# GateLoop attention with a maxout FFN: weight blocks fetched between the first gates' inputs and rounded ahead of the second group, the first FFN done block by block, and the second group without GpSimd

## Chip, cores, metric

One core of one Trainium2 chip. Times are device microseconds (us) of one execution; a median over a few executions is quoted with its lowest and highest.

## The reference

```python
# B, H, S, D = 4, 8, 768, 48
scale = np.minimum(mag, 0.999) / (mag + 1e-06)      # mag = |a|
for t in range(S):
    new_re = ar * S_re - ai * S_im                  # a complex state per head, D x D
    new_im = ar * S_im + ai * S_re
    S_re, S_im = new_re + k[t] (outer) v[t], new_im
    y[t] = q[t] @ S_re
x = y as (3072, 384)
h = max(x @ w1, x @ w2, x @ w3)                     # 384 -> 768
return h @ w_out                                    # 768 -> 384
```

The weights come as float64. The kernel reads each value as two int32 words and rounds it to float32 itself.

## The kernel before

The 3072 tokens are 24 tiles of 128. Two tiles are a group: group 0 is tiles 0 and 1, group 1 tiles 2 and 3, group 2 tiles 4 and 5. A group passes through *gates* (logarithm and angle of each a), *products* (decay of k and q), *angles* (prefix sums of the angles on TensorE, then sines), and then, for each tile, a *front* (transposes `turn`, decay factors `cut`, and `prep`, which makes Q, K, QB, KB, QG), the scores, the state and the outputs. An FFN step works a weight block against a tile's (later a group's) outputs. Tiles 0 and 1 have an FFN each, called FFN 0 and FFN 1 here; later FFNs take two tiles.

The gates:

```python
def gate_steps(g, cs):                      # cs: chunks (tiles) of the group
    def s0():
        # ... cut ...
        nc.scalar.activation(out=w, in_=ar, func=AF.Square)
        nc.scalar.activation(out=L, in_=ai, func=AF.Square)
        nc.vector.tensor_tensor(out=L, in0=L, in1=w, op=OP.add)
        nc.vector.tensor_scalar(out=L, in0=L, scalar1=SMALL, scalar2=LARGE, op0=OP.max, op1=OP.min)
        act(out=L, in_=L, func=AF.Ln)
    # ... s1 cut ...
    def s2():
        # ... cut ...
        (nc.gpsimd if g > 0 else nc.vector).tensor_tensor(out=ai, in0=ai, in1=L, op=OP.mult)
        nc.vector.tensor_tensor(out=w, in0=w, in1=L, op=OP.mult)
        nc.vector.scalar_tensor_tensor(out=w, in0=w, scalar=2.0, in1=ai, op0=OP.subtract, op1=OP.mult)
        # ... cut ...
    return [s0, s1, s2]
```

The rounding of one weight block, right behind its load:

```python
def load_weight(dst, src, i):
    # ... choice of the raw buffer cut ...
    nc.sync.dma_start(out=raw.rearrange("p n m w -> p n (m w)"), in_=src.bitcast(I32))
    low, high = raw[:, :, :, 0].bitcast(U32), raw[:, :, :, 1]
    ex = fp2.tile([P, n, m], I32, tag="xT", name="ex")
    nc.vector.tensor_scalar(out=ex, in0=high, scalar1=0x7FF00000, scalar2=None, op0=OP.bitwise_and)
    nc.scalar.activation(out=ex, in_=ex, func=AF.Relu, scale=8.0, bias=wbias)
    nc.vector.scalar_tensor_tensor(out=ex, in0=high, scalar=-0x80000000, in1=ex,
                                   op0=OP.bitwise_and, op1=OP.bitwise_or)
    nc.vector.tensor_scalar(out=high, in0=high, scalar1=0x000FFFFF, scalar2=None, op0=OP.bitwise_and)
    nc.scalar.activation(out=dst, in_=high, func=AF.Copy, scale=2.0 ** -20, bias=1.0)
    nc.vector.scalar_tensor_tensor(out=dst, in0=low, scalar=2.0 ** -52, in1=dst, op0=OP.mult, op1=OP.add)
    nc.vector.tensor_tensor(out=dst, in0=dst, in1=ex.bitcast(FP), op=OP.mult)
```

The order of the program. `weave` merges lists of steps, each over a stretch of the whole (0 to 1):

```python
load(0); load_v(0)
constants_early()                            # small masks on GpSimd
for t in us["k"] + us["q"] + fs + gs + vbs[2:]:
    nc.gpsimd.memset(t, 0.0)                 # the run of zero fills
weights = weight_steps()
# ... gates of group 0, chunk by chunk, and its first products ...
for f in weights[:3]: f()                    # blocks 0 to 2: load and round
load(1)
angles(0, list(range(C)))
# ... front of tile 0 ...
for g in range(NG):
    load_v(g + 1); load(g + 2)
    if g == 0:
        weave((0.0, 1.0, loop_steps(0)), (0.0, 0.7, weights[3:]), (0.15, 0.58, pre_steps(1)), (0.7, 1.0, ffn_steps([0])))
    else:
        ffn = ffn_steps(tokens(g * C - 1))
        # ...
        weave((0.0, 1.0, loop_steps(g)), (0.0, 0.7, pre_steps(g + 1, feed)),
              (0.0, 1.0 if g > 1 else 0.5, [call(feed, 1) for _ in ffn]))
```

So before, the gates and angles of group 1 are worked beside group 0's tiles, together with the rounding, and FFN 1 is spread over group 1's loop.

Of the kernel before, what the change touches and what calls it, by code (L numbers as in the profile page):

```python
# [9 lines left out]
FP = mybir.dt.float32  # L10
# [35 lines left out]
def kernel(  # L46
# [167 lines left out]
    def rows(a, g, c, lo=0, n=P):  # L214
        b, s = divmod(g, GB)
        t0 = (s * C + c) * P + lo
        return a[b, :, t0:t0 + n, :].rearrange("h t d -> t h d")

    def load(g):
        if g >= NG:  # L220
            return
        for nm, src in (("ar", a_re), ("ai", a_im)):
            T[nm, g] = ld2.tile([P, C, H, D], FP, tag=nm, name=nm)
        for c in range(C):
            for nm, src in (("ar", a_re), ("ai", a_im)):
                nc.sync.dma_start(out=T[nm, g][:, c], in_=rows(src, g, c))  # L226
        for c in range(C):
            x = g * C + c
            for nm, src in (("k", k), ("q", q)):
                T[nm, x] = ldx.tile([P, H, D], FP, tag=nm, name=nm)  # L230
                nc.sync.dma_start(out=T[nm, x], in_=rows(src, g, c))

    def load_v(g):
        if g >= NG:
            return
        for c in range(C):
            x = g * C + c
            T["v", x] = vbs[x % 4]
            for h in range(2):
                src = rows(v, g, c, h * L64, L64).rearrange("t (i u) d -> t i u d", u=2)  # L240
                for u in range(2):
                    nc.sync.dma_start(out=heads(T["v", x][h * L64:(h + 1) * L64, h])[:, :, u], in_=src[:, :, u])

    ws = [const.tile([P, KD, FF], FP, name="w%d" % i) for i in range(3)]
    wo = const.tile([P, KF, DM], FP, name="wo")

    def weight_steps():

        steps, n = [], FF // 3
        for f in range(3):  # L250
            for w, src in zip(ws, (moe_w1, moe_w2, moe_w3)):
                cols = slice(f * n, (f + 1) * n)
                steps.append(call(load_weight, w[:, :, cols], src.rearrange("(i p) m -> p i m", p=P)[:, :, cols], len(steps)))
        for f in range(0, KF, 2):
            view = moe_w_out.rearrange("(i p) m -> p i m", p=P)
            steps.append(call(load_weight, wo[:, f:f + 2], view[:, f:f + 2], 0))
        return steps

    def load_weight(dst, src, i):
        if src.dtype == FP:  # L260
            nc.sync.dma_start(out=dst, in_=src)
            return

        n, m = dst.shape[1:]
        if i % 3 == 2:

            raw = wo.bitcast(I32).rearrange("p f m -> p (f m)")[:, 0:2 * n * m].rearrange("p (n m w) -> p n m w", n=n, w=2)
        else:
            raw = fp2.tile([P, n, m, 2], I32, tag="hT", name="raw")
        nc.sync.dma_start(out=raw.rearrange("p n m w -> p n (m w)"), in_=src.bitcast(I32))  # L270
        low, high = raw[:, :, :, 0].bitcast(U32), raw[:, :, :, 1]

        ex = fp2.tile([P, n, m], I32, tag="xT", name="ex")
# [9 lines that stand above are left out]
# [9 lines left out]
    def gate_steps(g, cs):  # L292
# [27 lines left out]
        def s2():  # L320

            L, w, e, ar, ai = part("L"), part("w"), part("e"), part("ar"), part("ai")
            nc.scalar.activation(out=e, in_=ar, func=AF.Abs)
            nc.vector.tensor_tensor(out=w, in0=w, in1=e, op=OP.add)
            act(out=L, in_=w, func=AF.Ln)
            act(out=L, in_=L, func=AF.Exp, scale=-1.0)

            (nc.gpsimd if g > 0 else nc.vector).tensor_tensor(out=ai, in0=ai, in1=L, op=OP.mult)  # L328
            nc.vector.tensor_tensor(out=w, in0=w, in1=L, op=OP.mult)
            nc.vector.scalar_tensor_tensor(out=w, in0=w, scalar=2.0, in1=ai, op0=OP.subtract, op1=OP.mult)  # L330

            nc.scalar.activation(out=ar, in_=ar, func=AF.Sign, bias=tiny)
            nc.scalar.activation(out=ai, in_=ar, func=AF.Copy, scale=-0.25, bias=0.25)
            nc.scalar.activation(out=ar, in_=ar, func=AF.Copy, scale=-1.0 / math.pi)
            if lo == 0 and g % GB > 0:
                nc.gpsimd.tensor_tensor(out=ai[0:1, 0:DM], in0=ai[0:1, 0:DM], in1=T["carry", g], op=OP.subtract)
# [53 lines left out]
    def products(x):  # L390
        g, c = divmod(x, C)

        def sums(mat, nm):
            ps = psM.tile([P, DM], FP, tag="mm", padded_shape=[P, 512], name=nm)
            nc.tensor.matmul(out=ps, lhsT=mat, rhs=T["Ln", g][:, c * DM:(c + 1) * DM], start=True, stop=True)  # L395
            return ps

        def s0():

            ps = sums(mid, "mds")  # L400
            for nm, sg in (("k", 1.0), ("q", -1.0)):
                E = nat2.tile([P, DM], FP, tag="E", name="E")
                act(out=E, in_=ps, func=AF.Exp, scale=sg)
                eng = nc.gpsimd if g > 0 else nc.vector
                eng.tensor_tensor(out=hd(T[nm, x]), in0=E, in1=hd(T[nm, x]), op=OP.mult)  # L405

        def s1():
            for nm in "kq":
                u = T["U" + nm, x] = us[nm][x % len(us[nm])]
                nc.vector.tensor_tensor(out=u[:, :, :, 0:D], in0=T["CS", x], in1=two(hd(T[nm, x])), op=OP.mult)  # L410

        def s2():

            ps = sums(rest, "sfx")
            En = nat2.tile([P, DM], FP, tag="E", name="En")
            act(out=En, in_=ps, func=AF.Exp, scale=-1.0)
            u = T["Uk", x][:, :, :, 0:D]
            nc.vector.tensor_tensor(out=u, in0=u, in1=two(En), op=OP.mult)

        return s0, s1, s2  # L420


# [120 lines left out]
    def outputs(x, xs):  # L543
# [14 lines left out]
                                 lhsT=V[:, c, i, lo:lo + 32] if new else G[0:DD, c, i, lo:lo + 32],  # L558
                                 rhs=atm[:, h] if new else QG[0:DD, 2 * h + c], start=start, stop=stop)
        if x == xs[0]:  # L560
            T["xT", xs[-1]] = fp2.tile([P, KD, len(xs) * P], FP, tag="xT", padded_shape=[P, KD, TG], name="xT")
        o = (x - xs[0]) * P
        nc.scalar.copy(out=T["xT", xs[-1]][:, :, o:o + P], in_=y)  # L563

# [1 line left out]
    def up_step(xs, fp, i):  # L566
        xT, n = T["xT", xs[-1]], len(xs) * P
        if fp == 0 and i == 0:
            T["hT", xs[-1]] = fp2.tile([P, KF, n], FP, tag="hT", padded_shape=[P, KF, TG], name="hT")
        dst = T["hT", xs[-1]][:, 2 * fp:2 * fp + 2]  # L570
        ps = psM.tile([P, 2, n], FP, tag="mm", padded_shape=[P, 2, TG], name="up")
        for j in range(2):
# [19 lines left out]
    def call(f, *a):  # L592
        return lambda: f(*a)
# [18 lines left out]
        return [call(turn, x, 0), call(turn, x, 1)], [call(cut, x)], \  # L612
            [call(prep, x, p) for p in range(4)]

    def loop_steps(g):
        steps = []
        for x in range(g * C, (g + 1) * C):
            tr, ct, pr = front(x + 1)
            kt = [products(x + 1)[2]] if x + 1 < NX else []
            steps += [call(scores, x, "A"), call(gather, x, "A"), call(scores, x, "B")] + tr[:1]  # L620
            steps += [call(gather, x, "B"), call(state, x)] + tr[1:] + ct + pr[:1] + kt
            steps += [call(outputs, x, tokens(x))] + pr[1:]
        return steps

    table("natural_log_exp_and_others")
    for t in vbs[:2]:
        nc.gpsimd.memset(t, 0.0)
    load(0)
    load_v(0)
    constants_early()  # L630
    for t in us["k"] + us["q"] + fs + gs + vbs[2:]:
        nc.gpsimd.memset(t, 0.0)
    weights = weight_steps()
    for pair in zip(*(gate_steps(0, [c]) for c in range(C))):
        for f in pair:
            f()
    for c in range(C):
        products(c)[0]()
    for f in weights[:3]:
        f()  # L640
    load(1)
    angles(0, list(range(C)))
    constants_late()
    for f in [products(0)[1]] + sum(front(0), []) + [products(0)[2], products(1)[1]]:
        f()
    for g in range(NG):
        load_v(g + 1)
        load(g + 2)
        if g == 0:
            weave((0.0, 1.0, loop_steps(0)), (0.0, 0.7, weights[3:]), (0.15, 0.58, pre_steps(1)), (0.7, 1.0, ffn_steps([0])))  # L650
        else:
            ffn = ffn_steps(tokens(g * C - 1))

            def feed(n):
                for _ in range(min(n, len(ffn))):
                    ffn.pop(0)()

            weave((0.0, 1.0, loop_steps(g)), (0.0, 0.7, pre_steps(g + 1, feed)),
                  (0.0, 1.0 if g > 1 else 0.5, [call(feed, 1) for _ in ffn]))
    for f in ffn_steps(tokens(NX - 1)):  # L660
        f()

# [29 lines left out]
```

## Time and profile before

Before: 751.06 us median of 3 (749.87 to 751.43).

The prediction below shows the page and the stretches. A list of milestones of the profiled run, each the start of a TensorE group in its timeline:

| milestone | before |
|---|---|
| first prefix sum of group 0 | 34.24 |
| first prefix sum of group 1 | 88.1 |
| tile 2's first score product | 109.2 |
| first prefix sum of group 2 | 153.8 |
| tile 3's first score product | 155.9 |
| tile 4's first score product | 167.66 |
| end of the span | 748.2 |

How to read it: the last 580 us are TensorE's and the same in all kernels here, so a kernel is as fast as its tile 4 is early. And at the very start come the second chunk's addition and clamp. These are lines of VectorE's timeline before, and then of GpSimd's. A line of a timeline gives start and duration in us, engine, line of the kernel, operation, and in brackets the idle time before it and what ended it; PE is TensorE, DVE VectorE, ACT ScalarE and POOL GpSimd, and x2 is two instructions in one line.

```profile
7.57 0.56 DVE L307 TENSOR_TENSOR L<-L,w 128x384 f32<-128x384 f32 x1 [1.13 <-ACT L L306]
8.16 0.37 DVE L308 TENSOR_SCALAR L<-L 128x384 f32<-128x384 f32 x1
```

```profile
7.94 2.29 POOL L120 TENSOR_SCALAR_AFFINE_SELECT cuts<-cuts 128x4 f32<-128x4 f32 x14
10.17 1.83 POOL L632 MEMSET uk<- 128x1024 f32 x2
```

### The profile page before, as it was taken

The numbers are of one execution on the slowest core, as the hardware profiler recorded it, in microseconds if no ns is written. First come the engines' busy times: TensorE is split into PE (matmuls) and PEld (weight loads), VectorE is DVE, ScalarE is ACT, GpSimd is POOL, SyncE is SP. The second block draws the span as 40 slices with busy tenths as digits, with TensorE's granted clock in tenths as the row PEclk, the third lists the DMA queues.
The fourth block names the chain that finished last, engine by engine and source line by source line (L and its number), as shares of the span: only waits on it lengthen the run. The fifth ranks groups of instructions, "written<-read, shape, count | busy, mean of one in ns | idle before, by whom it ended". The sixth has DMA issues, their size and how long they took to land.

```text
span 748.2 us, 17645 instructions
## 1 busy us (share of the span) xinstructions
PE 670.9 (90%) x7620; PEld 543.1 (73%) x7620; DVE 518.4 (69%) x706; ACT 402.2 (54%) x677; POOL 130.4 (17%) x133
## 2 busy tenths in 40 slices
PE   1166279989999999999999999999999999999998
PEld 0054168968778878878878868878878878788785
DVE  4889997787866866866856867867857767655210
ACT  7595565666647546556556556556566465322010
POOL 9302400411302203102103103103004005000000
PEclk9986699999999999999999999999999999999999
DMA  9764430050220320320320420410410210000000
GB/s 173 156 178 136 121 92 23 8 103 10 54 65 11 56 66 9 74 51 7 72 54 6 77 52 5 91 35 7 91 33 10 46 33 2 1 23 2 12 11 22
DMA packets 134158, 38.91 MB, mean 52 GB/s; under 512 B 126784, under 2 KB 129856, under 8 KB 134080
## 3 DMA queue, kind: packets, MB, share of 16 engines
q1 hardware_dynamic: 133824, 37.76, 22.8%
q8 instruction: 60, 0.98, 0.6%
q14 instruction: 18, 0.15, 0.1%
q10 hardware_dynamic: 256, 0.01, 0.0%
HBM read 33.03 MB, written 4.72 MB: 50 GB/s over the span
## 4 chain that ended last, share of the span: by engine, by line
PE 73%; issue 11%; DVE 7%; ACT 4%; POOL 2%; SPq 2%; DMA 1%; ACTq 0%; POOLq 0%; DVEq 0%
PE up L575 35%; PE op L586 12%; PE tp L432 5%; PE dk L529 4%; PE B L492 4%; PE y L557 3%; PE A L492 2%; PE mds L395 2%; PE sfx L395 2%; PE F L445 2%; PE cs L350 2%; ACT e L106 1%; DVE QB L459 1%; SPq L226 1%; POOL ai L328 1%
## 5 line engine op out<-in xcount | busy, mean ns | idle before, releaser
L575 PE MATMUL up<-xT,w 128*128 128x256 f32 (+1 forms) x1404 | 299.3, 367 | 6.5 <-ACT xT L563 6.2
L575 PEld LDWEIGHTS up<-xT,w 128*128 128x128 f32 x1404 | 249.0, 191 | 46.4 <-ACT xT L563 7.7
L328 POOL TENSOR_TENSOR ai<-ai,L 128x768 f32<-128x768 f32 x11 | 30.4, 2759 | 418.4 <-ACT L L106 314.1
L586 PE MATMUL op<-wo,hT 128*128 128x384 f32 x288 | 97.9, 490 | 0.0
L580 DVE TENSOR_TENSOR hT<-hT,up 128x512 f32<-128x512 f32 (+1 forms) x78 | 49.9, 640 | 40.0 <-PE up L575 39.8
L586 PEld LDWEIGHTS op<-wo,hT 128*128 128x128 f32 x288 | 52.9, 190 | 33.3 <-DVE hT L580 0.5
L459 DVE TENSOR_TENSOR Q<-Q,f 112x512 f32<-112x512 f32 x48 | 40.3, 840 | 44.9 <-ACT f L106 44.9
L434 ACT COPY K<-tp 112x512 f32<-112x512 f32 x48 | 27.9, 581 | 60.0 <-PE tp L432 59.8
L578 ACT COPY hT<-up 128x512 f32<-128x512 f32 (+1 forms) x39 | 21.3, 548 | 69.6 <-PE up L575 68.6
L588 ACT COPY ot<-op 128x384 f32<-128x384 f32 x24 | 11.5, 477 | 81.5 <-PE op L586 81.5
L541 DVE TENSOR_TENSOR g<-g,dk 112x384 f32<-112x384 f32 x40 | 22.1, 552 | 47.0 <-PE dk L529 46.4
L350 PE MATMUL cs<-w,upto 128*128 128x384 f32 x48 | 20.5, 555 | 34.5 <-DVE w L346 34.5
L529 PEld LDWEIGHTS dk<-vb,uk 128*112 128x112 f32 x384 | 42.7, 183 | 9.9 <-issue 5.5
L557 PEld LDWEIGHTS y<-atm,vb 128*32 128x32 f32 x1536 | 39.7, 112 | 13.5 <-issue 8.4
L529 PE MATMUL dk<-vb,uk 128*112 128x96 f32 x384 | 43.1, 267 | 6.0 <-issue 5.2
L557 PE MATMUL y<-atm,vb 128*32 128x64 f32 x1536 | 47.1, 224 | 0.4 <-DVE atm L510 0.4
L557 PE MATMUL y<-QG,g 112*32 112x64 f32 x1536 | 46.5, 222 | 0.0
L459 DVE TENSOR_TENSOR QB<-Q,f 112x512 f32<-112x512 f32 (+1 forms) x48 | 46.3, 999 | 0.0
L405 POOL TENSOR_TENSOR k<-E,k 128x384 f32<-128x384 f32 x22 | 30.2, 1372 | 68.9 <-ACT E L106 65.2
L492 PE MATMUL A<-Q,K 112*64 112x96 f32 x768 | 38.7, 254 | 3.7 <-DVE Q L459 3.1
L492 PEld LDWEIGHTS A<-Q,K 112*64 112x64 f32 x768 | 33.9, 140 | 9.4 <-issue 5.2
L106 ACT ACTIVATE f<-F 48x296 f32<-48x296 f32 x96 | 39.6, 412 | 1.7 <-PE F L445 0.4
(107 smaller groups left out, 1126.9 us busy)
## 6 DMA issues: line engine op xcount, KB each, us to landing
ar<-in_a_re_dram SPq DMA_DIRECT2D x24, 192.0 KB, 3.6
ai<-in_a_im_dram SPq DMA_DIRECT2D x24, 192.0 KB, 4.0
k<-in_k_dram SPq DMA_DIRECT2D x24, 192.0 KB, 3.0
q<-in_q_dram SPq DMA_DIRECT2D x24, 192.0 KB, 3.0
vb<-in_v_dram SPq DMA_DIRECT2D x96, 48.0 KB, 2.4
raw<-in_moe_w_dram SPq DMA_DIRECT2D x6, 768.0 KB, 5.6
out_dram<-ot SPq DMA_DIRECT2D x24, 192.0 KB, 1.9
wo<-in_moe_w_dram SPq DMA_DIRECT2D x3, 768.0 KB, 6.4
```

The lines of the kernel that those rows point to most:

```text
L106: tab(nc.scalar.activation(**kw))
L328: (nc.gpsimd if g > 0 else nc.vector).tensor_tensor(out=ai, in0=ai, in1=L, op=OP.mult)
L350: nc.tensor.matmul(out=ps, lhsT=upto, rhs=w[:, c * DM:(c + 1) * DM], start=True, stop=c == 0)
L405: eng.tensor_tensor(out=hd(T[nm, x]), in0=E, in1=hd(T[nm, x]), op=OP.mult)
L432: nc.tensor.transpose(out=tp[0:DD, j], in_=both(T["U" + nm, x], hg * HU + j), identity=ident)
L459: nc.vector.tensor_tensor(out=out, in0=in_, in1=f.to_broadcast([DD, H, 2 * n, 8]), op=OP.mult)
L492: nc.tensor.matmul(out=ps[o:o + L64, h // HU, h % HU * 96:h % HU * 96 + 96], lhsT=K[0:DD, h, o:o + L64], rhs=Q[0:DD, 2 * h + c], start=Tru ...
L529: nc.tensor.matmul(out=ps[0:DD, h // HU, h % HU * 96:h % HU * 96 + 96], lhsT=both(T["Uk", x], h), rhs=T["v", x][:, :, h // 2, o:o + D], st ...
L557: nc.tensor.matmul(out=y[32 * (r % 4):32 * (r % 4) + 32, r // 4, c * L64:(c + 1) * L64], lhsT=V[:, c, i, lo:lo + 32] if new else G[0:DD, c ...
L575: nc.tensor.matmul(out=ps[:, j], lhsT=ws[i][:, d, f * P:(f + 1) * P], rhs=xT[:, d], start=(d == 0), stop=(d == KD - 1))
L580: nc.vector.tensor_tensor(out=dst, in0=dst, in1=ps, op=OP.max)
L586: nc.tensor.matmul(out=ps, lhsT=hT[:, f, o:o + P], rhs=wo[:, f], start=(f == 0), stop=(f == KF - 1))
```

## The change

The intent: the first weight blocks come in while the first gates are worked, so that all rounding is done before group 1 instead of running into it; FFN 0 starts while TensorE idles; and group 1's multiplies leave slow GpSimd. Three parts, cut to their core (the split of `load_weight` into `weight_load` and `weight_round`, the smaller load functions and the buffers for `raw`, `xT` and `hT` are left out):

```diff
-            (nc.gpsimd if g > 0 else nc.vector).tensor_tensor(out=ai, in0=ai, in1=L, op=OP.mult)
+            (nc.gpsimd if g > 1 else nc.vector).tensor_tensor(out=ai, in0=ai, in1=L, op=OP.mult)
...
-                eng = nc.gpsimd if g > 0 else nc.vector
+                eng = nc.gpsimd if g > 1 else nc.vector
...
-    load(0)
-    load_v(0)
+    blocks = weight_blocks()
+    for c in range(C):
+        load_a(0, c)
+        weight_load(c)
+    load_kq(0, 0)
+    weight_load(2)
+    load_kq(0, 1)
+    load(0, load_v)
+    for i in range(3, 7):
+        weight_load(i)
...
-    for f in weights[:3]:
-        f()
-    load(1)
+    for i in range(3):
+        weight_round(i)
+    load(1, load_a)
...
-            weave((0.0, 1.0, loop_steps(0)), (0.0, 0.7, weights[3:]), (0.15, 0.58, pre_steps(1)), (0.7, 1.0, ffn_steps([0])))
+    rounds = []
+    for i in range(3, len(blocks)):
+        rounds.append(call(weight_round, i))
+        if i + 4 < len(blocks):
+            rounds.append(call(weight_load, i + 4))
+    weave((0.0, 1.0, tile_steps(0)), (0.0, 1.0, rounds[:8]))
+    load(1, load_kq)
+    load(1, load_v)
+    ffn = ffn_steps([0])
+    weave((0.0, 1.0, ffn[:6] + rounds[8:12] + ffn[6:9] + rounds[12:] + ffn[9:]), (0.3, 1.0, gate_steps(1, list(range(C)))))
+    for f in tile_steps(1, False):
+        f()
+    ffn = ffn_steps([1])
...
+    weave((0.0, 1.0, pre_steps(1, feed)[3:] + sum(front(C), []) + [products(C)[2]]), (0.0, 1.0, [call(feed, 1)] * 5))
```

After it, group 1's gates stand behind most of the rounding, its angles and front behind tile 1, and FFN 1 is used up beside that front. The loops of groups 2 and later are as before.

## The prediction

> **What bounds the kernel now.** I read the page first, then busy time by stretch, then the VectorE and TensorE timelines of the first 170 us.
>
> ```profile
> span 748.2 us, 17645 instructions
> PE 670.9 (90%) x7620; PEld 543.1 (73%) x7620; DVE 518.4 (69%) x706; ACT 402.2 (54%) x677; POOL 130.4 (17%) x133
> ...
> PE   1166279989999999999999999999999999999998
> ...
> DVE  4889997787866866866856867867857767655210
> ...
> PEclk9986699999999999999999999999999999999999
> ```
>
> Each digit is 18.7 us. TensorE (PE) has 9s from the seventh slice on; before that it idles, at a reduced clock, while VectorE (DVE) has 8s and 9s. The averages (PE 90%) hide two kernels: a VectorE-bound start and a TensorE-bound rest. Stretches make that exact (busy us of each engine, then granted clock, DMA share, GB/s):
>
> ```profile
> 0.00:34.00 34.00, 3.27 (x4) 1.00 (x4) 21.46 (x47) 22.23 (x39) 23.69 (x67) 1.00 0.83 168
> 34.00:74.00 40.00, 26.81 (x318) 20.51 (x318) 36.84 (x53) 29.64 (x48) 3.02 (x1) 0.74 0.56 156
> 74.00:82.30 8.30, 0.00 (x0) 0.00 (x0) 6.70 (x5) 4.19 (x6) 6.32 (x5) 0.75 0.37 106
> 82.30:112.00 29.70, 18.52 (x166) 15.19 (x166) 29.61 (x43) 19.00 (x32) 2.18 (x1) 0.79 0.45 107
> 112.00:167.70 55.70, 53.33 (x788) 44.98 (x786) 43.59 (x66) 34.39 (x60) 10.42 (x6) 0.97 0.21 44
> 167.70:748.00 580.30, 569.00 (x6348) 461.41 (x6348) 380.23 (x497) 292.75 (x496) 84.72 (x54) 1.00 0.17 35
> ```
>
> From 167.7 us on PE is 98% busy at full clock: nothing in the start can shorten those 580 us, only move where they begin. I chose 167.7 because there the first score product of tile 4 (group 2) runs, and from that matmul on the PE order of the changed kernel is instruction for instruction that of the old one. So the question is one number: when does that product start?
>
> ```profile
> 167.66 1.54 PE L492 MATMUL A<-Q,K 112*64 112x96 f32 x32 [0.67 <-DVE Q L459]
> ```
>
> It waits for VectorE's Q. VectorE's queue is in order, and carries gates, the rounding of twelve float64 weight blocks (seven instructions each, five of them VectorE's), and the tiles. The worst place in it is where GpSimd takes part (start, duration):
>
> ```profile
> 70.98 4.59 POOL L328 TENSOR_TENSOR ai<-ai,L 128x768 f32<-128x768 f32 x1 [45.76 <-ACT L L106]
> 75.53 0.99 POOL L405 TENSOR_TENSOR k<-E,k 128x384 f32<-128x384 f32 x1
> ...
> 75.60 1.73 DVE L330 SCALAR_TENSOR_TENSOR w<-w,ai 128x768 f32<-128x768 f32 x1 [1.69 <-POOL ai L328]
> 77.26 1.74 DVE L282 TENSOR_TENSOR w<-w,ex 128x768 f32<-128x768 f32 x1
> 78.93 1.75 DVE L418 TENSOR_TENSOR uk<-uk,En 128x768 f32<-128x768 f32 x1
> 80.59 1.74 DVE L276 SCALAR_TENSOR_TENSOR ex<-raw,ex 128x768 int32<-128x768 int32 x1
> 82.26 1.21 DVE L459 TENSOR_TENSOR KB<-K,f 112x1024 f32<-112x1024 f32 x1
> ```
>
> VectorE waits 1.69 us for a GpSimd multiply of 4.59 us, and then four of its instructions take 1.74 us where the same shape elsewhere takes 0.95 (0.87 from start to start).
>
> **What the Trainium skill says.** "SBUF — State Buffer", section "SBUF: two separate sides": GpSimd and VectorE share a port pair, given as an exclusive lock, which a VectorE operation with two SBUF inputs takes against a GpSimd operation that reads SBUF. The trace agrees in kind: 1.74 against 0.95 us above. "GPSIMD Engine Reference", section 4.1, says two-input elementwise work is about 2x slower there; the trace has a 128x768 multiply at 2.59 us at its best (at 132.9 us) against 0.87 on VectorE, so nearer 3x. "TensorE: Matmul & The Clock Gate", Part 1: a starved TensorE runs at half clock and recovers after a few us of steady work. The trace agrees: twelve 128-wide up-products take 2.93 us at 112.1 and 1.50 us at 115.9, with clock 0.74 to 0.79 in the stretches before.
>
> **The change, part by part.** I take start-to-start times from VectorE's timeline where it was not held: 0.87 us for 128x768 with two inputs, 0.47 for 128x384 or a one-input 128x768, 0.60 and 1.14 for 112x512 and 112x1024, 0.62 and 0.33 for the masked copies, 0.33 for a 128x256 maximum.
>
> (1) *Group 1 without GpSimd.* Adds one 128x768 and four 128x384 multiplies to VectorE: 0.87 + 4 x 0.47 = 2.8 us. Removes the 1.69 us wait and 4 x (1.67 - 0.87) = 3.2 us of stretch. Net 2 us gained, and the gates' chain loses a 4.6 us link.
>
> (2) *Weight loads between the first gates' inputs.* Block 0 (768 KB) goes ahead of the second chunk of gates. The first 20 us ran at 188 GB/s, so 768 KB (0.79 MB) costs 4.2 us. Summing bytes in the new order, block 0 is there at about 8 us, the second chunk's gates at 10, block 1 at 14, block 2 at about 20. In the new VectorE order the first step of block 2's rounding stands ahead of the gates' multiplies, so those wait for its load. Walking the order with these arrivals, the second product of the angles (the w that the prefix sums wait for) is ready at 34.6 us; before, that instruction ended at 34.1. So nothing is gained at this point directly, but two of the first three blocks are by then rounded, which before happened between 25 and 39 us as well. About 0.
>
> (3) *First FFN block by block; rounding ahead of group 1.* No work is removed: the VectorE entries from the angles to tile 4's first Q sum to 105.4 us before and 108.2 us after (the 2.8 of part 1). Before, this took 165.4 - 34.1 = 131.3 us, so 25.9 us were waits and stretched instructions. What changes is how much of that remains. Six of FFN 0's nine up-steps can now run at about 68 us (tile 0's outputs at 64 to 67 us, weight blocks 0 to 5 rounded by then), into idle PE time, instead of at 99 to 116 us; the rounding ends at about 105 to 107 us instead of 123.2.
>
> My walk through the new VectorE order, with ScalarE's and PE's entries beside it, meets these waits: about 2.5 us where ScalarE's square of group 1's gates stands ahead of the angle's sines (those inputs come after 7 weight blocks, 8.1 MB, at 43 to 46 us) and for the factors f after it; about 5 us where VectorE's maxima of FFN 0 stand ahead of block 7's rounding (74 to 79 us, PE warming up); 3 to 4 us where k and q of group 1 wait for tile 1's and FFN 1's matmuls in PE's order; 3 us for prefix sums, sines and factors of group 1; 4 to 5 us of the same kind for group 2. Together 18 to 20 us against 25.9. Tile 4's first Q then stands at 34.6 + 108.2 + 18.5 = 161.3 us, and its product at 162, some 5.5 us before the old 167.66.
>
> PE as a check: from tile 2's second score product (about 129 us in my walk; 130.0 before, but with six of FFN 1's nine up-steps already done where before two were) to tile 3's outputs PE has some 26 us of work, so it cannot be there before 155 us. That would allow up to 10 us of gain, so VectorE's chain, not PE, decides.
>
> **The rivals.** *A: the whole wait goes.* If the walk is too pessimistic and most of the 18.5 us vanish, VectorE alone gives 34.6 + 108.2 = 143 us, PE about 150 to 155: 12 to 16 us gained, 735 to 739. For it: rounding ends 16 us earlier, and PE loses less to the half clock. Against it: the waits between prefix sums, sines and factors are chains over three engines that exist in every group. *B: nothing is gained.* DMA or ScalarE takes over: the first gates are delayed by weight loads, and ScalarE (18.1 us busy of 20 from 40 to 60 us) sits behind group 1's late inputs. Each would cost 3 to 6 us, leaving 748 to 753. For it: 0.91 DMA share in the first 20 us. Against it: before, VectorE's blocks 3 to 5 waited for buffers, which the new order loads early. *C: the gain comes back later,* because FFN 1 is used up early and cannot fill PE in group 1's loop, where VectorE has 37 us of work. Against it: group 2 and later have two-tile FFNs, the same in both.
>
> **Range and chances.** 5.5 us less, a shade more for the warmer clock: 745 us. Rival A weighs a fifth, B and C an eighth; range 736 to 752. Faster by over 2% means under 736.0, needing 15 us, nearly all of A: 0.13. Slower by 2% (over 766) needs a deadlock-like wait that I do not see: 0.03.
>
> **What would show it.** Right: from tile 4's first score product to the end about 580 us, unchanged; that product at about 162 us; last weight rounding near 106 us; up-products from about 68 us; no VectorE instruction of 1.7 us before 120 us; clock above 0.8 from 60 to 120 us. Wrong: angles' w later than 37 us (rival B, loads), a long ScalarE wait for group 1's a inputs between 40 and 50 us (B), PE idle of over 5 us in 112 to 165 us (C), or the product before 157 us (A).

## The result, and the profile after

After: 761.45 us median of 4 (760.09 to 762.24), before 750.46 beside it; ratio 1.0145, 95% interval 1.0121 to 1.0168. Slower by 11 us, within the 2% class, and outside my range. (A ratio here is the mean time of one kernel's runs over that of the other's of the same rounds, so not quite the ratio of the medians quoted.)

The page after:

```profile
span 760.5 us, 17637 instructions
...
PE 675.2 (89%) x7620; PEld 544.0 (72%) x7620; DVE 528.1 (69%) x711; ACT 400.9 (53%) x677; POOL 121.4 (16%) x128
...
PE   0167757978999999999999999999999999999998
...
DVE  6999984888866857867766866866857867755211
```

VectorE's busy time grew by 9.7 us though the change adds 2.8 us of work to it, and its seventh slice has a 4, where it had 7. TensorE got its early work as intended (7 and 7 in the fourth and fifth slices, 6 and 2 before), yet its unbroken 9s begin in the eleventh slice and not in the tenth. The stretches (columns as in the prediction), cut at the first prefix sums and at tile 4's product:

```profile
38.70:112.00 73.30, 49.80 (x612) 40.16 (x612) 67.66 (x104) 41.46 (x64) 4.29 (x10) 0.86 0.29 74
112.00:140.00 28.00, 21.61 (x181) 17.58 (x182) 15.39 (x22) 18.33 (x33) 0.00 (x0) 0.94 0.42 83
140.00:180.10 40.10, 31.41 (x482) 23.80 (x479) 33.70 (x47) 27.00 (x48) 9.58 (x6) 0.87 0.31 61
180.10:760.00 579.90, 569.15 (x6348) 461.44 (x6348) 381.01 (x496) 292.07 (x495) 85.05 (x54) 1.00 0.17 35
```

The last row is the old one, 579.9 us and the same 6348 matmuls. The loss lies ahead of it, in two places: the first prefix sum starts at 38.92 instead of 34.24, and from 112 to 140 us VectorE works 15.39 of 28 us and TensorE 21.61, where before both were fuller (20.48 and 27.95 in the same stretch of that kernel).

**The first place.** VectorE's timeline after:

```profile
7.95 0.95 DVE L285 TENSOR_SCALAR ex<-w 128x768 int32<-128x768 int32 x1 [1.42 <-DMA w<-in_moe_w_dram]
...
10.89 7.87 DVE L290 TENSOR_SCALAR w<-w 128x768 int32<-128x768 int32 x1
18.68 0.54 DVE L318 TENSOR_TENSOR L<-L,w 128x384 f32<-128x384 f32 x1
```

and GpSimd's, same kernel:

```profile
10.85 1.83 POOL L653 MEMSET uk<- 128x1024 f32 x2
...
17.27 2.12 POOL L653 MEMSET vb<- 128x1024 f32 x2
```

One mask instruction of the rounding, 0.55 to 0.69 us in the same form and shape elsewhere in this trace, occupies VectorE for 7.87 us. It starts as GpSimd's run of fills starts and ends in their last pair, itself a little longer than the others (2.12 against 1.84). The second chunk's addition, at 7.57 before, stands behind it and runs at 18.68.

**The second place.** VectorE's timeline after, at the front of group 1:

```profile
115.95 0.56 DVE L416 TENSOR_TENSOR k<-E,k 128x384 f32<-128x384 f32 x1 [4.23 <-ACT E L106]
...
122.59 0.55 DVE L367 SCALAR_TENSOR_TENSOR nf<-t,cs 128x384 f32<-128x384 f32 x1 [2.08 <-ACT t L365]
125.08 0.56 DVE L367 SCALAR_TENSOR_TENSOR nf<-t,cs 128x384 f32<-128x384 f32 x1 [1.94 <-DMA ar<-in_a_re_dram]
127.34 0.96 DVE L421 TENSOR_TENSOR uk<-CS,k 128x768 f32<-128x768 f32 x1 [1.71 <-ACT CS L106]
```

Products, prefix sums, sines: a chain that passes from TensorE to ScalarE to VectorE and back, and now VectorE has nothing else, because the rounding is done. Group 1's first prefix sum starts at 120.65 (88.1 before). (Where the bracket names a load, at 125.08, ScalarE's `t` had ended at 125.05, so that wait belongs to the chain too.) From the first prefix sum to tile 4's first score product VectorE is busy for 116.5 us in both kernels, but idle for 24.6 us after against 16.9 before: the loss in this place is idle time.

Theory: (i) a collision of a one-input VectorE instruction with GpSimd's fills, brought about by the load order, worth some 5 us; (ii) group 1's front, put behind the rounding, runs without work beside it, and what was gained ahead is lost there, some 8 us net. Rivals: the weight loads cost by their bytes; the GpSimd part is at fault; FFN 1, used up early, alone explains (ii).

### The profile page after: what moved, and what is told of

It reads as the page before. It is cut to its first block, busy times and chain, and to the rows that moved or that the text cites. A ratio compares the mean times of both kernels' runs of the same rounds, so it can differ in the third digit from the quotient of the medians. Undisturbed runs are those within 1.5% of the kernel's fastest.

```text
span 760.5 us, 17637 instructions
## 1 busy us (share of the span) xinstructions
PE 675.2 (89%) x7620; PEld 544.0 (72%) x7620; DVE 528.1 (69%) x711; ACT 400.9 (53%) x677; POOL 121.4 (16%) x128
## 4 chain that ended last, share of the span: by engine, by line
PE 72%; DVE 11%; ACT 8%; issue 5%; DMA 2%; POOL 1%; SPq 0%; ACTq 0%; DVEq 0%; POOLq 0%
PE up L590 35%; PE op L601 12%; PE dk L540 4%; PE tp L443 4%; PE B L503 4%; PE y L568 3%; PE A L503 2%; PE mds L406 2%; ACT e L106 2%; PE cs L361 2%; PE sfx L406 2%; PE F L456 2%; DVE w L290 1%; DVE Q L470 1%; DMA ai<-in_a_im_dram 1%
## 5 line engine op out<-in xcount | busy, mean ns | idle before, releaser
L601 PE MATMUL op<-wo,hT 128*128 128x384 f32 x288 | 99.8, 496 | 6.3 <-DVE wo L293 6.3
L339 POOL TENSOR_TENSOR ai<-ai,L 128x768 f32<-128x768 f32 x10 | 25.0, 2504 | 367.6 <-ACT L L106 294.1
L470 DVE TENSOR_TENSOR Q<-Q,f 112x512 f32<-112x512 f32 x48 | 41.9, 874 | 45.7 <-ACT f L106 45.6
L406 PE MATMUL mds<-Ln,mid 128*128 128x384 f32 x48 | 23.2, 568 | 24.2 <-DVE Ln L329 23.4
L443 PE MATMUL tp<-ident,uk 128*112 128x128 f32 x192 | 30.3, 282 | 11.1 <-DVE uk L421 10.9
```

Of the source, the lines that this page charges most:

```text
L339: (nc.gpsimd if g > 1 else nc.vector).tensor_tensor(out=ai, in0=ai, in1=L, op=OP.mult)
L406: nc.tensor.matmul(out=ps, lhsT=mat, rhs=T["Ln", g][:, c * DM:(c + 1) * DM], start=True, stop=True)
L443: nc.tensor.transpose(out=tp[0:DD, j], in_=both(T["U" + nm, x], hg * HU + j), identity=ident)
L470: nc.vector.tensor_tensor(out=out, in0=in_, in1=f.to_broadcast([DD, H, 2 * n, 8]), op=OP.mult)
L601: nc.tensor.matmul(out=ps, lhsT=hT[:, f, o:o + P], rhs=wo[:, f], start=(f == 0), stop=(f == KF - 1))
```

## The experiments

Thirteen kernels. Stretch means: from the first prefix sum to tile 4's first score product. Each batch ran beside the kernel before on the same chip (medians 750.76, 751.41, 751.54, 750.98), always 4 executions of the new kernel.

### The GpSimd part alone, and undone

`b_nopool` is the kernel before with

```diff
-  nc.gpsimd if g > 0 else nc.vector
+  nc.gpsimd if g > 1 else nc.vector      # both places
```

and `a_pool` the changed kernel with the reverse.

> The kernel before with one part of the change alone: group 1's five multiplies on VectorE, not GpSimd. Theory (as predicted): VectorE is the bound from 34 to 112 us, so the 1.69 us wait and 3.2 us of stretched instructions go and 2.8 us of work come; 1.5 to 3 us faster, about 748. Rival: the waits only move, time within 0.7 us of before. Rival: VectorE pays the 2.8 us and ScalarE or PE sets the end of the stretch, 2 us slower. In the profile: no VectorE instruction of 1.7 us between 70 and 85 us.

Measured 748.3 (747.95 to 748.57), ratio 0.9962 [0.9932, 0.9992]. First prefix sum 34.34, tile 4 at 166.29, stretch 131.95 against 133.42.

> The changed kernel with that one part undone: group 1's five multiplies on GpSimd again. Theory: they cost what they cost before, 2 us or more slower than the changed kernel (763 to 765). Rival: in the new order the VectorE waits of group 1 (13 us idle from 112 to 140) hide them, and the time stays within 1 us of 761.5, or even falls.

Measured 763.1 (762.25 to 763.81), ratio 1.016 [1.0133, 1.0187]: 1.7 us over the changed kernel, with overlapping intervals (1.0121 to 1.0168 there). The traces do not put this difference where the multiplies are: a_pool's stretch is 140.4 us against 141.2, and its first prefix sum comes 0.9 us later (39.86), at the start that the edit leaves alone. So this part is a gain of about 2 us in the kernel before; in the changed kernel a gain is not shown, and the rival, that the waits of group 1 hide the multiplies, fits the traces. It is not the culprit.

### Rounding held back behind the first gates

`a_hold` is the changed kernel with one order constraint more:

```diff
-        nc.vector.tensor_scalar(out=ex, in0=high, scalar1=0x7FF00000, ...)
+        first = nc.vector.tensor_scalar(out=ex, in0=high, scalar1=0x7FF00000, ...)
+        if i < 3:
+            tc.add_manual_dep(first.ins, T["gate", 0].ins.name, order, reason="rounding after the first gates")
```

> The changed kernel with the first rounding step of weight blocks 0 to 2 ordered behind the first gates' last VectorE step; loads as in the change. Theory A (collision): the 7.87 us rounding step at 10.9 us was held up by GpSimd's back-to-back zero fills; with the gates ahead of it nothing of the sort stands before the gates, the w that the prefix sums wait for is ready at 33 to 35 us, not 38.7, and the whole is 3 to 5 us faster than the changed kernel (757 to 758). Theory B (loads): the weight loads between the inputs delay the gates; then that w stays at 37 us or later. Theory C: the start does not matter, later waits absorb it, and the time stays within 1 us of 761.5.

Measured 766.54 (763.03 to 768.03), ratio 1.02 [1.0163, 1.0236]; the first prefix sum at 42.90, later still. The hoped-for repair failed, for a reason that tells more than success would have. VectorE's timeline of a_hold:

```profile
10.04 0.56 DVE L320 TENSOR_TENSOR L<-L,w 128x384 f32<-128x384 f32 x1 [3.81 <-ACT L L319]
10.63 7.95 DVE L321 TENSOR_SCALAR L<-L 128x384 f32<-128x384 f32 x1
```

With the rounding out of the way the *gates' own clamp* meets the fills and takes 7.95 us, 0.37 before. Not what the rounding does, but that some one-input instruction stands there, is what costs (the next run narrows down which ones). And it stands there because block 0's load ahead of the second chunk moved that chunk's addition from 7.57 to 10.04.

### The collision taken away without moving a load

`a_noclash` is the changed kernel with the clamp of group 0 and both masks of blocks 0 and 1 in a form with two inputs (the same tensor twice; the upper clamp is left out for group 0, the result stays correct):

```diff
-  nc.vector.tensor_scalar(out=high, in0=high, scalar1=0x000FFFFF, scalar2=None, op0=OP.bitwise_and)
+  nc.vector.scalar_tensor_tensor(out=high, in0=high, scalar=0x000FFFFF, in1=high, op0=OP.bitwise_and, op1=OP.bitwise_and)
...
+  nc.vector.scalar_tensor_tensor(out=L, in0=L, scalar=SMALL, in1=L, op0=OP.max, op1=OP.max)   # g == 0
```

> The changed kernel with the one-input VectorE steps of the first 20 us (the clamp of the first gates, the two bit masks of weight blocks 0 and 1) written as two-input instructions with the same result (the upper clamp is left out for group 0; these inputs never reach it). Theory A (collision on a shared port, as held_up one-input steps of 7.9 us during GpSimd's zero fills show in the changed kernel and in the kernel with rounding held back): the two-input form doesn't wait for fills, no VectorE instruction of over 2 us before 20 us, the prefix sums start at 33 to 35 us and not 38.9, time 756 to 758. Rival: any VectorE instruction waits while GpSimd fills; then a step of 7 to 8 us appears again and the time stays at 761.

Measured 756.88 (755.76 to 757.42), ratio 1.0062 [1.0045, 1.0079]; first prefix sum 32.96. VectorE's timeline of a_noclash:

```profile
10.75 0.96 DVE L294 SCALAR_TENSOR_TENSOR w<-w 128x768 int32<-128x768 int32 x1
...
12.22 0.59 DVE L326 SCALAR_TENSOR_TENSOR L<-L 128x384 f32<-128x384 f32 x1
```

The same mask at nearly the same moment takes 0.96 instead of 7.87 us, though undisturbed this form is the slower one (0.96 against 0.55 to 0.69). The first prefix sum comes 6 us earlier; the time falls by 4.6. That is place (i), shown. The stretch stays at 141.5, so place (ii) is untouched.

The two masks did not meet the same GpSimd work, though. GpSimd's timeline of a_noclash, and what VectorE then runs beside the fills:

```profile
8.14 4.71 POOL L120 TENSOR_SCALAR_AFFINE_SELECT cuts<-cuts 128x4 f32<-128x4 f32 x14
12.80 1.84 POOL L662 MEMSET uk<- 128x1024 f32 x2
```

```profile
13.60 0.95 DVE L286 SCALAR_TENSOR_TENSOR ex<-w 128x768 int32<-128x768 int32 x1
...
15.34 0.54 DVE L338 SCALAR_TENSOR_TENSOR Ln<-L,e 128x384 f32<-128x384 f32 x1
...
17.92 0.94 DVE L288 TENSOR_SCALAR ex<-w 128x768 int32<-128x768 int32 x1
```

At 10.75 GpSimd was still making small masks, which took 4.71 us here and 2.87 in the changed kernel, so that the fills began 2 us later. How much of the gain is the form and how much the later fills was not separated. But the instructions with two inputs that do run beside the fills, as those at 13.60 and 15.34, are not held up. Neither is the one-input mask at 17.92. It takes 0.94 us without GpSimd too (0.95 at 24.88 in the changed kernel); the same source line takes 0.55 where the raw block lies in a buffer of its own. So the instructions held up in these runs are one-input instructions of the fast kind (0.37 us for the clamp and 0.55 to 0.69 for the mask undisturbed, 7.55 to 7.95 beside the fills), and not every one-input instruction.

The Trainium skill, "SBUF — State Buffer", section "Who interferes with whom", has the rule: one-source instructions such as `tensor_scalar` can, with suitable operands, run in a mode that takes VectorE's second port pair, which GpSimd shares, and then the one that is late "fully blocks"; an instruction with two SBUF inputs contends with GpSimd's reads, not with an instruction that only writes. The trace agrees on both: 7.87 us for the fast mask of the changed kernel, and 0.95 and 0.54 us for two inputs, beside fills, which only write.

### The load order undone, and the load order alone

`a_loads`: the changed kernel with all inputs of the first gates ahead of the weights.

```diff
-    for c in range(C):
-        load_a(0, c)
-        weight_load(c)
-    load_kq(0, 0)
-    weight_load(2)
-    load_kq(0, 1)
-    load(0, load_v)
-    for i in range(3, 7):
+    load(0, load_a, load_kq, load_v)
+    for i in range(7):
         weight_load(i)
```

> The changed kernel with the loads in the order of before (all inputs of group 0, then the weights). Theory: the second chunk's clamp runs at 8 us again, before the run of zero fills from 10 us on, so the prefix sums start at 33 to 35 us, time 756 to 758: 4 to 5 us less than the changed kernel, and still 5 us more than before, because of group 1's late front. Rival: the later weights delay FFN 0 and the rounding, and the time stays at 760 or more.

Measured 757.08 (755.75 to 758.09), ratio 1.0066 [1.0047, 1.0085]: 4.4 us below the changed kernel. The second chunk's clamp ran at 8.29 for 0.37 us, ahead of the fills; first prefix sum 34.66, tile 4 at 174.59.

`b_loads`: the kernel before with the loads of blocks 0 to 2 between the inputs (into columns of the weight tiles that are still free), the rounding in its old place in the program.

> The kernel before with one part of the change alone: the loads of weight blocks 0 to 2 between the first gates' inputs, rounding in its old place in the program. Theory: the same VectorE order of the first 20 us results as in the changed kernel, a one-input step waits some 8 us for GpSimd's fills, the prefix sums start at 38 to 40 us, and as VectorE is the bound until 112 us nearly all of it reaches the end: 754 to 756. Rival: earlier weights make up for it, within 1 us of 750.5.

Measured 759.28 (753.18 to 759.89), ratio 1.0071 [1.0024, 1.0117], above the 754 to 756 expected; first prefix sum 39.85. VectorE's timeline of b_loads:

```profile
11.25 7.65 DVE L285 TENSOR_SCALAR w<-w 128x768 int32<-128x768 int32 x1
```

So the load order alone, in a kernel with nothing else of the change, makes the collision. The profiled execution took 759.54; one of the four took 753.18, without a trace of its own, so that it escaped the collision is likely but not shown. The stretch in b_loads was 137.5, four us more than before; VectorE's busy time in it is the same (116.95 against 116.51), so it is waiting, but for what I did not find. It is not the loads as such, as c_before_best below shows.

With a_loads and b_nopool a third comparison comes free: both load the inputs first and both have no GpSimd in group 1, so they differ in the order of rounding, FFN and group 1, with the buffers and the earlier loads of later blocks that go with it. 757.08 against 748.3: **part 3 by itself costs 8.8 us.** The three parts, each by its own pair of runs: -2.5 (GpSimd, before to b_nopool), +8.8 (order, b_nopool to a_loads), +4.4 (loads, a_loads to after). That they add up is no check, because the four kernels form a chain. Pairs of different batches also carry up to 1 us by which the medians of the kernel before differ.

### Which piece of the order

Two things could make group 1's front slow: its gates come late (behind the rounding), or FFN 1 is used up beside it. `a_gates1early` weaves the gates of group 1 into tile 0 again and puts its next steps beside FFN 0; `a_ffn1late` keeps FFN 1 for group 1's loop (and gives its `hT` another buffer, a line that is left out below and was not tested by itself):

```diff
# a_gates1early
-    weave((0.0, 1.0, tile_steps(0)), (0.0, 1.0, rounds[:8]))
+    weave((0.0, 1.0, tile_steps(0)), (0.0, 1.0, rounds[:8]), (0.3, 1.0, gate_steps(1, list(range(C)))))
...
-    weave((0.0, 1.0, ffn[:6] + ... ), (0.3, 1.0, gate_steps(1, list(range(C)))))
+    weave((0.0, 1.0, ffn[:6] + ... ), (0.0, 1.0, pre_steps(1)[3:]))
...
-    weave((0.0, 1.0, pre_steps(1, feed)[3:] + sum(front(C), []) + [products(C)[2]]), (0.0, 1.0, [call(feed, 1)] * 5))
+    weave((0.0, 1.0, sum(front(C), []) + [products(C)[2]]), (0.0, 1.0, [call(feed, 1)] * 5))
# a_ffn1late
-    weave((0.0, 1.0, pre_steps(1, feed)[3:] + sum(front(C), []) + [products(C)[2]]), (0.0, 1.0, [call(feed, 1)] * 5))
+    for f in pre_steps(1)[3:] + sum(front(C), []) + [products(C)[2]]:
+        f()
```

> The changed kernel with group 1's gates woven into tile 0 and the rest of group 1's front (sums, angles) into FFN 0, not behind them; loads, block-wise FFN 0 and no GpSimd kept. Theory (late chain): the changed kernel lost because group 1's front is a chain over three engines that now runs from 80 to 130 us with nothing beside it on VectorE (13 us idle from 112 to 140 us); with rounding and tile 1 beside it the first score product of tile 4 comes at 165 to 170 us, not 180.1, and the time is 746 to 752. Rival (filler): PE lacks FFN 1 as filler in group 1's loop, where A and B of tile 3 and the prefix sums are waited for; this kernel also uses FFN 1 up early, so it gains little, 757 or more.

Measured 758.96, ratio 1.0092 [1.0049, 1.0136], but its executions lie at 753.78, 758.09, 759.84 and 760.28.

> The changed kernel with FFN 1 kept for group 1's loop (fed there over its first half, as before), not used beside group 1's front. Theory (filler): the changed kernel has PE idle 8.7 us from 140 to 180 us at clock 0.87 because FFN 1 is gone by then; kept back, PE idles more from 112 to 140 us and less after; if filler in the loop is what counts, the first score product of tile 4 comes 3 us or more before 180.1, time 755 to 758. Rival (VectorE's chain): VectorE's own waits set that point, so it moves by less than 1.5 us either way, or PE's extra work in the loop delays it by 2 to 5 us.

Measured 758.1, ratio 1.0079 [1.0039, 1.0119], at 755.1, 755.64, 760.57 and 760.73.

Both are inconclusive: the spread of one kernel is as large as the effect that was to be measured. The profiled execution of each was its fastest, and in it the mask of L290 took 1.44 and the clamp of L319 3.21 us, not 7.87: the same collision, in a milder form, with the first prefix sum at 35.0. Since both edits leave the start of the program alone, the degree of it is not the edit's doing. VectorE's timeline of a_gates1early, then GpSimd's:

```profile
10.61 1.44 DVE L290 TENSOR_SCALAR w<-w 128x768 int32<-128x768 int32 x1
...
12.54 3.21 DVE L319 TENSOR_SCALAR L<-L 128x384 f32<-128x384 f32 x1
```

```profile
8.00 3.97 POOL L120 TENSOR_SCALAR_AFFINE_SELECT cuts<-cuts 128x4 f32<-128x4 f32 x14
11.91 1.84 POOL L653 MEMSET uk<- 128x1024 f32 x2
```

Four traces with this start point to what decides: who is first. In the two mild ones the mask starts at 10.57 and 10.61, while GpSimd is still making small masks; in the changed kernel and a_pool it starts at 10.89 and 11.35, when the fills have begun (10.85 and 10.08). Block 0's first mask, which waits for its load, starts at 7.60 and 7.66 in the mild ones against 7.95 and 8.40. So in these traces some 0.3 us in the arrival of a load separate 35.0 from 38.9 us. That the executions without a trace differ for this reason is likely, not shown. To see the order alone, the collision has to go first. So both were repeated on top of a_noclash (the first with both of its moves, although its expectation says "and nothing else" than the gates):

> a_noclash (756.9 us, stretch from the first prefix sum to tile 4's first score product 141.5 us) with the gates of group 1 worked beside tile 0, and nothing else: FFN 1 is still used up beside group 1's front. With FFN 1 late as well it ran in 744.6 with a stretch of 129.5, so the two together are worth 12. Additive halves: 750 to 751.5, stretch about 135.5. If the gates' place is nearly all of it: 745 to 747. If FFN 1's place is nearly all of it, or each helps only with the other: 754 to 757.

Measured 753.57 (751.61 to 756.79), ratio 1.0032 [1.0007, 1.0057].

> a_noclash with FFN 1 kept for group 1's loop, and nothing else: the gates of group 1 stay behind the rounding, beside FFN 0. Additive halves: 750 to 751.5, stretch about 135.5. If the gates' place is nearly all of the 12 us: 754 to 757. If FFN 1's place is: 745 to 747. If each is worth little without the other, both runs come out at 754 to 757.

Measured 754.81 (753.73 to 755.08), ratio 1.0055 [1.004, 1.0069]. Neither is near the 750 to 751.5 of additive halves; the second lies where "each is worth little without the other" has it, the first just below, with its fastest execution at 751.61.

And both together, on top of a_noclash (`c_noclash_g1_late`) and of a_loads (`c_loads_g1_late`), run before those two:

> As c_loads_g1_late, but the weight loads stay between the inputs as in the change, and the collision is taken away by writing the first gates' clamp and the masks of weight blocks 0 and 1 as instructions with two inputs (as in a_noclash). Theory: the same as for c_loads_g1_late with w at about 33 us, so the product at about 166 us and the time 747 to 750 us: the loads' place costs nothing once no one-input instruction meets the fills. Rival (the loads' place costs by itself, through the DMA queues): w at 33 but c_noclash_g1_late at least 3 us above c_loads_g1_late.

Measured **744.57** (743.55 to 745.9), ratio 0.9907 [0.9878, 0.9935]; first prefix sum 32.91, tile 4 at 162.45, stretch 129.5. Under the range that I expected by 2.4 us (its stretch was to be 133), and the fastest kernel.

> The changed kernel with three things undone at once: all inputs of the first gates are loaded before any weight block (as in the run a_loads), the gates of group 1 are worked beside tile 0 (as in a_gates1early), and FFN 1 is kept for group 1's loop (as in a_ffn1late). Rounding and FFN 0 stay ahead of group 2. Theory (two separate costs, a collision of VectorE's one-input step with GpSimd's fills at the start, and group 1's front worked late with nothing beside it): w for the prefix sums at 33 to 34.7 us, no one-input VectorE instruction over 1.5 us before 21 us, the stretch from the first prefix sum to tile 4's first score product about 133 us, that product at about 167 us, the time 747 to 751 us. Rival (the two repairs of group 1's front help against the same wait, so do not add, or the rounding on its own ahead of group 2 costs the rest): stretch 136 to 138 us, time 753 to 755 us.

Measured 748.9 (748.07 to 749.44), ratio 0.9962 [0.994, 0.9984]; first prefix sum 34.52, tile 4 at 166.40, stretch 131.9. The theory's numbers, and equal to b_nopool's 748.3: with the two repairs the 8.8 us of part 3 are gone.

From a_noclash's 756.88 the gates alone are worth 3.3 us (5.3 by their fastest execution), FFN 1 alone 2.1, both 12.3. They do not add; each is worth most with the other. The milestones show how (profiled runs):

| | a_noclash | + FFN 1 late | + gates early | + both | before |
|---|---|---|---|---|---|
| first prefix sum of group 0 | 32.96 | 32.59 | 33.71 | 32.91 | 34.24 |
| of group 1 | 114.5 | 112.3 | 86.0 | 85.3 | 88.1 |
| tile 2's first score product | 131.0 | 129.6 | 125.7 | 117.5 | 109.2 |
| first prefix sum of group 2 | 159.2 | 157.8 | 156.9 | 147.0 | 153.8 |
| tile 4's first score product | 174.44 | 172.22 | 174.65 | 162.45 | 167.66 |
| VectorE idle in the stretch | 25.7 | 24.2 | 25.3 | 14.2 | 16.9 |

In all five VectorE is busy for 115.3 to 116.5 us of the stretch; what differs is how long it is idle, and only the pair shortens that by more than 2 us.

With late gates tile 2 waits for the chain through the angles, and where FFN 1 stands matters by about 1 us only. With early gates that chain starts its prefix sums at 86 us, long before the rounding ends, and tile 2 could start as soon as the rounding is over. But if FFN 1 is fed there, TensorE works it first, in order. TensorE's timeline of d_noclash_gates1, then VectorE's:

```profile
114.45 2.93 PE L599 MATMUL up<-xT,w 128*128 128x128 f32 x12 [0.95 <-ACT xT L585]
...
120.20 0.72 PE L465 MATMUL F<-cuts,Ln 128*48 128x74 f32 x16
120.85 4.29 PE L599 MATMUL up<-xT,w 128*128 128x128 f32 x36
...
125.72 1.46 PE L512 MATMUL A<-Q,K 112*64 112x96 f32 x30
```

```profile
120.38 0.42 DVE L604 TENSOR_TENSOR hT<-hT,up 128x256 f32<-128x256 f32 x1 [9.27 <-PE up L599]
122.69 0.69 DVE L479 TENSOR_TENSOR Q<-Q,f 112x512 f32<-112x512 f32 x1 [1.89 <-ACT f L106]
```

VectorE waits 9.27 us for an FFN block and makes Q for tile 2 behind it at 122.69. With both repairs that Q is made at 115.06, and FFN 1's blocks come between the scores of group 1's loop instead (VectorE's timeline of c_noclash_g1_late):

```profile
115.06 0.69 DVE L479 TENSOR_TENSOR Q<-Q,f 112x512 f32<-112x512 f32 x1 [3.72 <-ACT f L106]
...
121.77 0.40 DVE L604 TENSOR_TENSOR hT<-hT,up 128x256 f32<-128x256 f32 x1
```

From 112 to 140 us VectorE is then busy for 23.07 us and TensorE for 27.80, against 15.39 and 21.61 in the changed kernel. Why d_noclash_gates1 spreads over 5 us between executions, with its profiled one the slowest, I did not settle; in the table its column is that slowest one.

### The old order with the harmless parts

`c_before_best` is b_loads with the two-input forms of a_noclash and without GpSimd in group 1:

> The kernel before, in its own order of tiles, rounding and FFN, with the three parts that did no harm by themselves: weight blocks 0 to 2 loaded between the first gates' inputs (as in b_loads), the first clamp and the masks of blocks 0 and 1 as two-input instructions so that they do not meet the fills, and no GpSimd multiplies in group 1 (as in b_nopool). Theory: w at 33 to 34 us, the stretch from there to tile 4's first score product about 132 us, that product at about 165.5 us, the time 745 to 748.5 us, so at or a little under b_nopool's 748.3. Rival (early loads also cost through the queues or the stretch, as b_loads's stretch of 137.5 us could mean): time 753 or more.

Measured 747.11 (746.59 to 747.36), ratio 0.9938 [0.9917, 0.996]; first prefix sum 33.27, tile 4 at 164.67, stretch 131.4. So early weight loads are harmless in the old order too, once nothing collides: 1.2 us better than b_nopool, of another batch. In the new order they are worth 4.3 us (744.57 against 748.9). And rounding and FFN 0 ahead, the heart of the change, does pay 2.5 us (744.57 against 747.11), if group 1's gates stay early and FFN 1 late.

## Why the prediction was wrong

- **"From tile 4's first score product to the end about 580 us"**: right, 579.9, in all kernels.
- **Part 1, GpSimd, "net 2 us gained"**: right for the kernel before, 2.5 by b_nopool (1.5 in its stretch); in the changed kernel not shown. Between 21 and 120 us no VectorE instruction of over 1.3 us is left in the timeline after; the one that breaks the sign "of 1.7 us before 120 us" is the mask of 7.87.
- **Part 2, loads, "About 0"**: wrong, +4.4 us. I had the arrival of the second chunk right ("at 10"; a_hold's addition ran at 10.04). I predicted the angles' w at 34.6; it was ready just before 38.92. The failed step is the walk's flat duration of 0.47 us for a one-input instruction, whatever GpSimd does beside it: one took 7.87. I had cited the port rule only for instructions with two inputs, and its part on one input, with the fills' place in GpSimd's timeline, would have warned me. The check that I had named for rival B ("later than 37 us") fired, but its cause was not the bytes: a_noclash has the same loads and a w before 33.
- **Part 3, "18 to 20 us against 25.9" of waits and stretched instructions**: wrong, and the largest miss. Counted the same way, 180.10 - 38.92 - 108.2 leaves 33.0 up to the product, where I allowed 18.5 up to Q and 0.7 from there. That is 13.8 too many, and with the 4.3 of part 2 (38.92 against 34.6) it gives the 18.1 us between the predicted 162 and the measured 180.10. Of the 33.0, 24.6 are idle time of VectorE and 8.3 are instructions that took longer than the walk's durations. The walk had waits and stretched instructions shrink together; idle time grew by 7.7 us instead (16.9 before). The terms that failed, as far as they are known:
  - "3 us for prefix sums, sines and factors of group 1". The timeline above shows 2.08, 1.94 and 1.71 us for these alone, with 4.23 for k ahead of them (I had 3 to 4 there) and more for FFN 1's maxima between. I counted each hand-over once and took the rest as overlapped, but after the rounding nothing was left to overlap with.
  - Group 2's GpSimd multiplies, which still stretch VectorE, were not in the walk at all. VectorE's timeline after:

```profile
151.29 1.74 DVE L341 SCALAR_TENSOR_TENSOR w<-w,ai 128x768 f32<-128x768 f32 x1 [1.71 <-POOL ai L339]
152.96 1.48 DVE L470 TENSOR_TENSOR Q<-Q,f 112x512 f32<-112x512 f32 x1
154.36 2.01 DVE L470 TENSOR_TENSOR KB<-K,f 112x1024 f32<-112x1024 f32 x1
```

  Undisturbed, w takes 0.95, Q 0.69 and KB 1.22 in this trace. From w's start at 151.29 to QG's at 161.11 these and the Q, uk and two QB (0.60 and 1.14) between take 4.0 us more than by the prediction's start-to-start times.
  - The rest of the 13.8, some 7 us, was not assigned to single terms.
- **FFN 0's earlier start**: it came as predicted (up-products from 70.92 against "about 68", last rounding at 110.6 against 105 to 107) and did warm TensorE (clock 0.86 from 38.7 to 112 us). It did not bring the time, because TensorE was not the limit there.
- **Rival C, argued away** because group 2 and later are the same: wrong argument. Of the 18.1 us 7.5 fall in group 1's loop, ahead of group 2, and its sign, TensorE idle for over 5 us from 112 to 165 us, came true (6.4 us from 112 to 140 alone). From tile 2's second score product (139.57; I had said 129) to tile 4's first it took 40.5 us, where I allowed 33; the trace has TensorE at a clock of 0.87 and busy for 31.41 of 40.1 us there. But C alone is half a cause: FFN 1 late without early gates brought 2.1 us. The full cause is the pair, shown by the four runs of the last table.

Two sums of the prediction are off without changing this: the waits of the walk add to 17.5 to 19.5 us, not 18 to 20, and a product at 150 to 155 us (rival A) would have meant 13 to 18 us gained, not 12 to 16.

So the mechanism of the gain was real, and worth 2.5 us; what I missed were two costs that its own order brought along, of 4.4 and some 12 us. That c_noclash_g1_late lies at the predicted 745 us is chance: it is another kernel, and the prediction did not foresee either repair.

## What to carry to other kernels

Before interposing a load or moving a step, look at what the *other* engine on the shared ports does at the new moment: a fast one-input VectorE instruction (0.37 to 0.69 us here) that falls into a run of GpSimd fills can cost the whole run (up to 7.95 us here), and writing it with two inputs was a cheap cure. Work that is moved forward leaves a hole behind: a chain over three engines that used to run beside it then runs alone, so move the chain's first steps (here group 1's gates) forward too and keep fillers (here FFN 1) back. Two repairs that look weak one by one may be strong together; test the pair, and take out any source of spread first.

## What the Trainium skill lacked or had wrong

- "SBUF — State Buffer", section "Who interferes with whom", says that the late one blocks while the other's instruction holds the ports. It does not say that a VectorE instruction can be kept out across a whole back-to-back run: 7.87, 7.95 and 7.65 us here, in the changed kernel over four pairs of fills of 1.1 to 1.8 us each and part of a fifth. Nor is it always kept out to the end: 3.21 us in a_gates1early, where the fills ran on to 20.4 us.
- The section does not name the cure that its own rule gives, a two-input form: with it the first prefix sum came at 32.96 instead of 38.92 us.
